# First slots of an attention and SwiGLU kernel: own buffers for weight chunks, and another placing of products

## The chip, the cores and the metric

The kernel runs on one core of a Trainium2 chip. The time is device microseconds of one execution, from its first to its last instruction. TensorE (PE) multiplies matrices, VectorE (DVE), ScalarE (ACT) and GpSimd (POOL) work elementwise, and SyncE (SP) issues most of the transfers. PEld is TensorE's loading of weights, which overlaps its matmuls.

## The reference

Two attention steps over 32 inducing points, then an RMS norm and a gated feed-forward network. Setup and reference, cut:

```python
B, N, m, C = (4, 12416, 32, 128)           # attention; d_ff = 1536, 49664 tokens in all
def mab(q, kv):
    s = scale * (q @ kv.transpose(0, 2, 1))
    s = s - s.max(-1, keepdims=True)
    a = np.exp(s)
    a /= a.sum(-1, keepdims=True) + 1e-09
    return a @ kv
h = mab(I, x)
y = mab(x, h)                              # reshaped to (49664, 128)
# ...
xn = y / np.sqrt(np.mean(y * y, axis=-1, keepdims=True) + 1e-06) * rms_g
g = xn @ w_gate
silu = g * (1.0 / (1.0 + np.exp(-g)))
return (silu * (xn @ w_val) @ w_out).astype(np.float32)
```

The three weight matrices arrive as 64-bit floats. The kernel turns them into 32-bit ones itself, in nine chunks of 128x512: (0,c) of the gate, (1,c) of the value, (2,c) of the output weights, c = 0, 1, 2.

## The kernel before

The second attention and the network are joined: the weights of the network's first layer are multiplied with h once per batch (the stacks sg and sv), so that a block of up to 512 tokens needs only its normalised attention weights a. A **unit** is such a block; a **slot** is one of its 12 groups of 128 hidden channels. There are 4 x 25 x 12 = 1200 slots. In a slot TensorE projects twice, ScalarE takes the silu, VectorE multiplies, and later TensorE adds the **product** with the output weights:

```python
def slot(j, products, steps, tanh):
    products(0)
    g = bank()
    nc.tensor.matmul(g[:, 0:T], sg[:, ts(j, P)], a[:, 0:T], start=True, stop=True)      # L681
    # ... silu on ScalarE: L689
    products(1)
    v = bank()
    nc.tensor.matmul(v[:, 0:T], sv[:, ts(j, P)], a[:, 0:T], start=True, stop=True)      # L692
    # ... VectorE multiplies silu with v: L698
    steps()
    if (b, u, j) in kinds:
        soon(1, lambda: three(j, t))
    else:
        plain.append(lambda: project(wo[:, j, :], t[:, 0:T]))
```

A **plain** product is one matmul of 32-bit floats (L617). A **three** splits both operands into parts and does three faster matmuls (L637, L639 and L617) after work on ScalarE, VectorE and GpSimd (L663 to L673). Two of the three add up in one PSUM bank, u3; when the last one of a unit is in, ScalarE copies it out (L642).

`steps()` does all other work of the kernel that has been given to this slot: rounding chunks, scores, exponentials, the sums of the next batch. In the first slots it is this:

```python
for k, one in ((1, (2, 1)), (5, (0, 2)), (8, (1, 2)), (11, (2, 2))):       # rounding of four chunks
    for j, name in ((0, "power"), (1, "power_number"), (1, "upper"), (2, "upper_number"), (2, "sign"), (3, "lower")):
        add(k + j, weight[one][name])
for k, *one in ((2, 0, 1), (4, 1, 1), (11, 0, 2), (13, 1, 2)):
    add(k, f["stack_of"], *one)        # L471: chunk times h, into a stack
    add(k, f["stack_low"], *one)
```

Rounding ends with `lower`: VectorE joins the parts (L281), GpSimd multiplies and writes the chunk (L283), and SP copies it to DRAM for later batches (L221). Where the chunk lies is chosen in `power`:

```python
if not c:
    t = silp.tile([P, 512], F32, name="silu") if i else halves.tile([P, 512], F32, name="lo")
    w0[i, c] = t[:]
else:
    if (0, 1) not in w0:
        w0["home"] = xnp.tile([P, 4, 512], F32, name="xn1")
    w0[i, c] = w0["home"][:, 2 * (c - 1) + i, :]
```

The places xn1 to xn4 hold rows of x before that. Later xn2, xn3 and xn4 hold the parts hi, lo and d of the threes.

Which products go into which slot, and which of them are threes, is planned ahead in `rehearse()`, which adds up fixed durations per engine (`run` puts work on an engine's clock) and only writes lists:

```python
def has(kind, by):
    return bool(queues[kind]) and queues[kind][0][0] <= by

def fill(to, until):
    while until > at["PE"] + 0.25:
        now = at["PE"] + 0.05
        kind = next((kind for kind in ("three", "plain") if has(kind, now)), None)
        if kind is None:
            break
        issue(kind, to)

# do(name), one step's cost
for e, us in zip(ENGINES, cost):
    if us:
        t = run(e, us, t, free[i]) if e == "PE" and i is not None else run(e, us, t)

# in a slot
least = 1 if near(b, k, 0, 4) or (b, u) == flat[-1] else RESERVE + 2 * near(b, k, -2, 0)     # RESERVE is 7
choose(second, min(2, max(0, split["all"] - least + 1)))
```

`choose` issues products while at least `least` are outstanding; `fill` issues more where TensorE would wait for a bank.

Of the kernel before, what the change touches and what calls it, by code (L numbers as in the profile page):

```python
# [23 lines left out]
def kernel(  # L24
# [189 lines left out]
    def rounding(i, c):  # L214


        st = {}

        def put():
            if i < 2:  # L220
                nc.sync.dma_start(out=w32[i][c][:], in_=st["dst"])  # L221
            if unread:
                fetch_raw(*unread.pop(0))

        def numbers(name, add, mul, engine):

            t, to = st[name], st[name] if name == "e" else st[name].bitcast(F32)
            if engine is nc.scalar and name == "e":
                nc.scalar.activation(to[:], t[:], AF.Relu, bias=bias, scale=mul)
            elif engine is nc.scalar:  # L230
                nc.scalar.activation(to[:], t[:], AF.Copy, bias=add, scale=mul)
            else:
                engine.tensor_scalar(out=to[:], in0=t[:], scalar1=mul, scalar2=add, op0=ALU.mult, op1=ALU.add)

        def power():
            if i < 2:
                if not c:
                    t = silp.tile([P, 512], F32, name="silu") if i else halves.tile([P, 512], F32, name="lo")
                    w0[i, c] = t[:]
                else:  # L240
                    if (0, 1) not in w0:
                        w0["home"] = xnp.tile([P, 4, 512], F32, name="xn1")
                    w0[i, c] = w0["home"][:, 2 * (c - 1) + i, :]
                dst = st["dst"] = w0[i, c]
            else:
                dst = st["dst"] = wo.rearrange("p j c -> p (j c)")[:, ts(c, 512)]
            if not wide:
                nc.sync.dma_start(out=dst if i < 2 else dst.rearrange("p (j c) -> p j c", c=C), in_=source(i, c))
                return
            words = raw[i, c].rearrange("p (f w) -> p f w", w=2)  # L250
            st["low"], st["high"] = words[:, :, 0], words[:, :, 1]
            e = st["e"] = work.tile([P, 512], I32, name="we", tag="work")
            nc.vector.tensor_scalar(out=e[:], in0=st["high"], scalar1=20, scalar2=0x7FF,
                                    op0=ALU.logical_shift_right, op1=ALU.bitwise_and)

        def power_number(engine=nc.scalar):
            if wide:
                e = st["e"]
                if engine is not nc.scalar:
                    nc.vector.tensor_scalar(out=e[:], in0=e[:], scalar1=896.0, scalar2=1151.0, op0=ALU.max, op1=ALU.min)  # L260
                numbers("e", -896.0 * (1 << 23), float(1 << 23), engine)

        def upper():
            if wide:
                f = st["f"] = outp.tile([P, 512], I32, name="o")
                nc.vector.tensor_scalar(out=f[:], in0=st["high"], scalar1=0xFFFFF, scalar2=None, op0=ALU.bitwise_and)

        def upper_number(engine=nc.scalar):
            if wide:
                numbers("f", 1.0, 2.0 ** -20, engine)  # L270

        def sign():
            if wide:
                e = st["e"]
                nc.vector.scalar_tensor_tensor(out=e[:], in0=st["high"], scalar=-(1 << 31), in1=e[:],
                                               op0=ALU.bitwise_and, op1=ALU.bitwise_or)

        def lower():
            if wide:
                e, f = st["e"], st["f"].bitcast(F32)  # L280
                nc.vector.scalar_tensor_tensor(out=f[:], in0=st["low"].bitcast(U32), scalar=2.0 ** -52, in1=f[:],  # L281
                                               op0=ALU.mult, op1=ALU.add)
                nc.gpsimd.tensor_tensor(out=st["dst"], in0=f[:], in1=e.bitcast(F32)[:], op=ALU.mult)  # L283
            put()

        return dict(locals())
# [516 lines left out]
    if B > 1:  # L803
        for _ in range(R):
# [7 lines left out]
            "power": (0, .45), "power_number": (0, 0, .63), "upper": (0, .6), "upper_number": (0, 0, .53), "sign": (0, .6),  # L812
            "lower": (0, .6, 0, 1.26), "stack_of": (.87, 0, .5), "stack_low": (0, .62), "split_wo": (0, 0, .7, 1.52)}
    BANKS = {"scores1", "sum_h", "max2", "max3", "fold_l", "turn_h", "square_h", "stack", "scores2", "square", "stack_of"}
    ENGINES = ("PE", "DVE", "ACT", "POOL")
    TAIL = {"PE": .17, "DVE": .09, "ACT": .11, "POOL": .04}
    MADE = {"sums": ((-.16,), (0, .6, .49), (0, 0, 0, 1.25)), "differences": ((-.16,), (0, 0, .53, 1.25), (0, 0, .52, 1.25))}
# [113 lines left out]
    def rehearse():  # L931

        at = dict.fromkeys(ENGINES, 0.0)
        free, open_banks = [0.0] * 5, {}
        taken = [0.0] * SILU
        queues, uses, later, left = {"plain": [], "three": []}, [0], [], {}
        split = {"out": 0, "u3": 0.0, "all": 0, "made": 0}

# [4 lines left out]
        def bank():  # L943
            return free.index(min(free))
# [2 lines left out]
            later.append([k, step])  # L947

        def has(kind, by):
            return bool(queues[kind]) and queues[kind][0][0] <= by  # L950

        def ready():
            return sum(one[0] <= at["PE"] for q in queues.values() for one in q)
# [1 line left out]
        def issue(kind, to):  # L955
            to.append(kind)
            t, unit, w = queues[kind].pop(0)[:3]
            split["all"] -= 1
            st = left[unit]
            if kind == "plain":  # L960
                end = run("PE", 0.858 * w, t)
            else:
                if st["three"] == 0:
                    run("PE", 0, split["u3"])
                end = run("PE", 0.697 * w, t)
                split["out"] -= 1
                split["made"] -= 1
                st["three"] += 1
                st["open"] -= 1
            st["left"] -= 1  # L970
            st["end"] = end
            if not st["left"] and st["all"]:
                close(unit, w)

        def close(unit, w):
            st = left[unit]
            if st["three"]:
                split["u3"] = run("ACT", 0.47 * w, st["end"])

            def finish():  # L980
                run("DVE", 0.6 * w, st["end"], split["u3"])
                soon(1, lambda: run("DVE", 0.63 * w))

            soon(1, finish)
# [19 lines left out]
                    break  # L1004
                issue(kind, to)

        def do(name):
            cost = COST.get(name, ())
            t = 0.0
            if name == "turn_z" or name == "stack_low":  # L1010
                i, t = open_banks[name].pop(0)
                free[i] = run("DVE", 0.61, t)
                if name == "turn_z":
                    run("DVE", 0.63)
                return
            i = bank() if name in BANKS else None
            for e, us in zip(ENGINES, cost):
                if us:
                    t = run(e, us, t, free[i]) if e == "PE" and i is not None else run(e, us, t)
            if name in ("square", "stack_of"):  # L1020
                open_banks.setdefault("turn_z" if name == "square" else "stack_low", []).append((i, t))
                free[i] = 1e9
            elif i is not None:
                free[i] = t
# [24 lines left out]
        def slot(b, k, u, j, tanh):  # L1049
            w = per2[units[u][0]] * m / 512.0  # L1050
            st = left.setdefault((b, u), dict(left=NJ, three=0, open=0, all=False, slots=0, end=0.0))
            kind = decide(b, k, u, j)
            first, second = picks[b, k] = [], []
            gi = bank()
            fill(first, free[gi])
            g = run("PE", 0.2325 * w, free[gi])
# [1 line left out]
            if tanh:  # L1058
                silu = run("DVE", 0.6 * w, silu)
            free[gi] = silu  # L1060
            least = 1 if near(b, k, 0, 4) or (b, u) == flat[-1] else RESERVE + 2 * near(b, k, -2, 0)
            choose(second, min(2, max(0, split["all"] - least + 1)))
            if kind != "sums":
                uses[0] += 1
# [12 lines left out]
            while any(not one[0] for one in later):  # L1077
                one = next(one for one in later if not one[0])
                later.remove(one)
                one[1]()  # L1080
            names = [step.__name__ for step, _ in given(b, k, u, j)]
            for name in names:
                if name in ("exp1_of", "exp2") and k in plans[b][1]:
                    run("ACT", 1.28)
                do(name)
            if near(b, k, 2, 3):
                run("ACT", 1.28)
            if kind:
# [23 lines left out]
            st["slots"] += 1  # L1112
            if st["slots"] == NJ:
                st["all"] = True
                if not st["left"]:
                    close((b, u), w)

# [7 lines left out]
    for b in range(B):  # L1125
# [3 lines left out]
        for k, (u, j) in slots(b):  # L1129

            def steps():

                for one in waiting:
                    one[0] -= 1
                while any(not one[0] for one in waiting):
                    one = next(one for one in waiting if not one[0])
                    waiting.remove(one)
                    one[1]()
                for step, args in given(b, k, u, j):
                    step(*args)  # L1140
                if j == (6 if (b, u) == (0, R - 1) else 2) and (b or u > 1) and (b, u) in after:
                    gather(*after[b, u])

            def products(some):
                for kind in picks[b, k][some]:
                    (plain if kind == "plain" else kara).pop(0)()

            if u not in unit:
# [36 lines left out]
```

## Time and profile before

| | |
|---|---|
| time, median of 3 runs | 1638.86 us (1637.6 to 1640.44) |
| span of the profiled execution | 1635.7 us |
| granted TensorE clock | 1.00 |
| first slot's first projection | 55.12 us after the start |
| scores in the steps of slot 18 | 84.67 us |

Busy columns of a window are time in which an engine had an instruction open; for TensorE the ends are modelled and overlap, so the spacing of starts tells its work better. A releaser in brackets is the instruction whose end came last before the waiting one began; it is inferred.

### The profile page before, as it was taken

Reading aid. Unit: us, or ns where it says so; the run is one execution under the profiler, and the core shown is the slowest. Engines: PE = TensorE matmul, PEld = TensorE weight load, DVE = VectorE, ACT = ScalarE, POOL = GpSimd, SP = SyncE. Lnnn points to the kernel's source line nnn. Section 1 sums busy time; section 2 is a strip of 40 time slices with the busy share of each in tenths; the row PEclk is TensorE's granted clock in tenths of the full one; section 3 lists DMA queues with packets and bytes.
Section 4 is the critical chain, followed back from the end, with each engine's and each line's share of the span. In section 5 each row is a group of like instructions: output and inputs, shape, how many; then the busy total and the mean of one; then the engine's idle time right before and its main releaser. Section 6 shows DMA issues by size and latency. Waiting matters only on the chain.

```text
span 1635.7 us, 25441 instructions
## 1 busy us (share of the span) xinstructions
PE 1608.4 (98%) x7086; PEld 1084.5 (66%) x7086; DVE 1444.4 (88%) x2506; ACT 1246.0 (76%) x2285; POOL 1217.5 (74%) x979
## 2 busy tenths in 40 slices
PE   8899999999999999999999999999999999999998
PEld 6546666766676666765667666676567776677776
DVE  4878988899899997889899998789989999999997
ACT  4567888767787778777778787777778788778786
POOL 1348895878588886688767897577858878878876
PEclk9999999999999999999999999999999999999999
DMA  6455534433454241624335324253221122112211
GB/s 260 90 72 81 90 62 85 102 90 63 65 88 69 40 88 26 135 58 103 63 67 84 57 39 87 49 131 77 51 38 29 29 40 38 34 35 38 39 36 27
DMA packets 389181, 112.52 MB, mean 69 GB/s; under 512 B 365072, under 2 KB 369712, under 8 KB 386480
## 3 DMA queue, kind: packets, MB, share of 16 engines
q1 hardware_dynamic: 388304, 110.82, 34.6%
q8 instruction: 56, 0.92, 0.2%
q14 instruction: 85, 0.70, 0.2%
q10 hardware_dynamic: 736, 0.08, 0.0%
HBM read 53.95 MB, written 27.00 MB: 49 GB/s over the span
## 4 chain that ended last, share of the span: by engine, by line
PE 85%; DVE 4%; issue 3%; ACT 2%; POOL 2%; DMA 1%; SPq 0%; DVEq 0%; ACTq 0%; POOLq 0%
PE acc L617 31%; PE gv L681 16%; PE gv L692 15%; PE u L637 9%; PE u L639 9%; PE gv L326 3%; PE gv L503 1%; DVE gv L698 1%; PE gv L382 1%; ACT silu L689 1%; DVE u L698 1%; POOL rs L520 1%; POOL xn L673 1%; DVE xn L664 1%; PE gv L457 0%
## 5 line engine op out<-in xcount | busy, mean ns | idle before, releaser
L673 POOL TENSOR_TENSOR xn<-xn,xn 128x512 fp32r<-128x512 f32 (+2 forms) x706 | 872.0, 1255 | 305.9 <-DVE xn L664 169.5
L689 ACT ACTIVATE silu<-gv 128x512 f32<-128x512 f32 (+2 forms) x1186 | 691.5, 586 | 271.9 <-PE gv L681 242.5
L692 PE MATMUL gv<-a,sv 128*128 128x512 f32 (+2 forms) x1188 | 634.9, 534 | 2.4 <-ACT silu L689 2.2
L681 PE MATMUL gv<-a,sg 128*128 128x512 f32 (+2 forms) x1188 | 489.6, 412 | 1.9 <-ACT silu L689 0.8
L617 PE MATMUL acc<-u,wo 128*128 128x512 f32 (+2 forms) x988 | 489.5, 580 | 0.0
L698 DVE TENSOR_TENSOR u<-silu,gv 128x512 f32<-128x512 f32 (+1 forms) x619 | 407.3, 664 | 53.9 <-PE gv L692 33.3
L698 DVE TENSOR_TENSOR gv<-silu,gv 128x512 f32<-128x512 f32 (+2 forms) x567 | 378.5, 669 | 77.0 <-PE gv L692 55.7
L664 DVE SCALAR_TENSOR_TENSOR xn<-xn,gv 128x512 fp32r<-128x512 f32 (+2 forms) x568 | 373.1, 657 | 9.0 <-ACT xn L663 6.2
L663 ACT ACTIVATE xn<-gv 128x512 fp32r<-128x512 f32 (+2 forms) x568 | 332.2, 585 | 41.3 <-DVE gv L698 31.2
L681 PEld LDWEIGHTS gv<-a,sg 128*128 128x128 f32 x1188 | 223.7, 188 | 187.2 <-ACT silu L689 40.4
L692 PEld LDWEIGHTS gv<-a,sv 128*128 128x128 f32 x1188 | 223.7, 188 | 142.6 <-issue 48.9
L617 PE MATMUL acc<-xn,more 128*128 128x512 f32 (+2 forms) x706 | 275.1, 390 | 6.1 <-POOL xn L673 2.9
L637 PE MATMUL u<-xn,xn 128*128 128x512 f32 (+2 forms) x706 | 272.9, 387 | 0.9 <-ACT o L642 0.7
L617 PEld LDWEIGHTS acc<-u,wo 128*128 128x128 f32 x988 | 184.6, 188 | 46.3 <-issue 9.4
L668 POOL TENSOR_TENSOR xn<-u,xn 128x512 fp32r<-128x512 f32 (+1 forms) x138 | 177.3, 1285 | 5.4 <-ACT xn L667 5.4
L639 PE MATMUL u<-xn,xn 128*128 128x512 f32 (+2 forms) x413 | 159.8, 387 | 0.1
L617 PEld LDWEIGHTS acc<-xn,more 128*128 128x128 f32 x706 | 132.5, 188 | 40.8 <-POOL xn L673 13.4
L637 PEld LDWEIGHTS u<-xn,xn 128*128 128x128 f32 x706 | 132.7, 188 | 31.2 <-issue 4.6
L639 PE MATMUL u<-xn,more 128*128 128x512 f32 (+2 forms) x293 | 113.3, 387 | 0.0
L667 ACT ACTIVATE xn<-u 128x512 fp32r<-128x512 f32 (+1 forms) x138 | 87.0, 630 | 30.0 <-DVE u L698 23.1
L520 POOL TENSOR_TENSOR rs<-ms,mhalf 128x16 f32<-128x16 f32 (+2 forms) x28 | 75.9, 2710 | 25.2 <-DVE ms L515 24.8
L639 PEld LDWEIGHTS u<-xn,xn 128*128 128x128 f32 x413 | 77.5, 188 | 17.5 <-POOL xn L668 0.5
(151 smaller groups left out, 1092.2 us busy)
## 6 DMA issues: line engine op xcount, KB each, us to landing
out_dram<-o SPq DMA_DIRECT2D x320, 64.0 KB, 2.0
xT<-in_x_dram SPq DMA_DIRECT2D x60, 256.0 KB, 5.1
xn<-in_x_dram SPq DMA_DIRECT2D x60, 256.0 KB, 4.9
a<-hi SPq DMA_DIRECT2D x156, 64.0 KB, 2.0
a<-lo SPq DMA_DIRECT2D x156, 64.0 KB, 2.0
xn<-in_x_dram SPq DMA_DIRECT2D x5, 1024.0 KB, 10.2
xn<-w SPq DMA_DIRECT2D x18, 256.0 KB, 3.5
out_dram<-o SPq DMA_DIRECT2D x64, 60.0 KB, 2.0
```

Source lines behind the costliest of these rows:

```text
L520: nc.gpsimd.tensor_tensor(out=rs, in0=st["ms"], in1=mhalf[rows, 0:n], op=ALU.pow)
L617: nc.tensor.matmul(acc[:, 0:T], lhsT, rhs, start=st["left"] == NJ, stop=st["left"] == 1)
L637: nc.tensor.matmul(ups[:, 0:T], weight_of(0, j), hi, start=st["k"] == nk, stop=False)
L639: nc.tensor.matmul(ups[:, 0:T], weight_of(1, j), lo, start=False, stop=not st["k"])
L663: nc.scalar.activation(hi, v, AF.Copy, scale=(1.0 - 2.0 ** -13) * 2.0 ** -12)
L664: nc.vector.scalar_tensor_tensor(out=lo, in0=hi.bitcast(F32), scalar=-4096.0, in1=v, op0=ALU.mult, op1=ALU.add)
L668: nc.gpsimd.tensor_tensor(out=lo, in0=v, in1=d.bitcast(F32), op=ALU.subtract)
L673: nc.gpsimd.tensor_tensor(out=d, in0=hi.bitcast(F32), in1=lo.bitcast(F32), op=ALU.subtract)
L681: nc.tensor.matmul(g[:, 0:T], sg[:, ts(j, P)], a[:, 0:T], start=True, stop=True)
L689: nc.scalar.activation(sl[:, 0:T], g[:, 0:T], AF.Silu)
L692: nc.tensor.matmul(v[:, 0:T], sv[:, ts(j, P)], a[:, 0:T], start=True, stop=True)
L698: nc.vector.tensor_tensor(out=t[:, 0:T], in0=sl[:, 0:T], in1=v[:, 0:T], op=ALU.mult)
```

## The change

It gives each of the four later gate and value chunks a buffer of its own. Before slot 16 of the first batch, products are issued from three outstanding on instead of seven. The plan now knows when a step's operand is made (`AFTER`, `done`), and in front of a step's matmul it places products until the operand is due; the kernel issues these right ahead of that step. The plan also takes ScalarE's copy of u3 where the last three of a unit is issued, and holds a unit's first three back until that copy is over. No instruction is added or taken out by the placing; only order and the choice between plain and three can change.

The diff, cut:

```diff
         def power():
             if i < 2:
-                if not c:
-                    t = silp.tile([P, 512], F32, name="silu") if i else halves.tile([P, 512], F32, name="lo")
-                    w0[i, c] = t[:]
-                else:
-                    if (0, 1) not in w0:
-                        w0["home"] = xnp.tile([P, 4, 512], F32, name="xn1")
-                    w0[i, c] = w0["home"][:, 2 * (c - 1) + i, :]
+                t = (xnp.tile([P, 512], F32, name=f"xn{2 * c - 1 + i}") if c else
+                     silp.tile([P, 512], F32, name="silu") if i else halves.tile([P, 512], F32, name="lo"))
+                w0[i, c] = t[:]
# ... (AFTER, done, rounded)
         def has(kind, by):
-            return bool(queues[kind]) and queues[kind][0][0] <= by
+            if not queues[kind]:
+                return False
+            t, unit = queues[kind][0][:2]
+            if kind == "three" and not left[unit]["three"]:
+                t = max(t, split["u3"])
+            return t <= by
# ... issue(): a three
-                if st["three"] == 0:
-                    run("PE", 0, split["u3"])
                 end = run("PE", 0.697 * w, t)
# ...
+                st["end"] = end
+                copy(st, w)
# ...
+        def copy(st, w):
+            if st["all"] and st["three"] and not st["open"] and "u3" not in st:
+                st["u3"] = split["u3"] = run("ACT", 0.47 * w, st["end"])
+
         def close(unit, w):
             st = left[unit]
-            if st["three"]:
-                split["u3"] = run("ACT", 0.47 * w, st["end"])
# ... do()
-            t = 0.0
+            t = done.get(args if name == "stack_of" else AFTER.get(name), 0.0)
             i = bank() if name in BANKS else None
             for e, us in zip(ENGINES, cost):
+                if us and e == "PE":
+                    t = max(t, free[i])
+                    fill(to, t)
                 if us:
-                    t = run(e, us, t, free[i]) if e == "PE" and i is not None else run(e, us, t)
+                    t = run(e, us, t)
+            done[rounded[step] if step in rounded else name] = t
# ... slot()
-            least = 1 if near(b, k, 0, 4) or (b, u) == flat[-1] else RESERVE + 2 * near(b, k, -2, 0)
+            least = (1 if near(b, k, 0, 4) or (b, u) == flat[-1] else 3 if not b and k < 2 * NJ - 8 else
+                     RESERVE + 2 * near(b, k, -2, 0))
# ... the kernel's own loop
-                for step, args in given(b, k, u, j):
+                for n, (step, args) in enumerate(given(b, k, u, j)):
+                    products(n + 2)
                     step(*args)
```

More of the change, by code (lines that the diff above doesn't have):

```diff
@@ L814 @@
     BANKS = {"scores1", "sum_h", "max2", "max3", "fold_l", "turn_h", "square_h", "stack", "scores2", "square", "stack_of"}
+    AFTER = {"max2": "max1", "max3": "max2", "fold_l": "exp1_of", "turn_h": "divide", "square_h": "turn_h", "square": "turn_a",
+             "sum_h": "turn_e", "scores1": "turn_x", "stack": "turn_h", "root": "scale", "apply": "root"}
     ENGINES = ("PE", "DVE", "ACT", "POOL")
@@ L934, in rehearse @@
         free, open_banks = [0.0] * 5, {}
-        taken = [0.0] * SILU
+        taken, done = [0.0] * SILU, {}
+        rounded = {weight[one]["lower"]: one for one in chunks}
         queues, uses, later, left = {"plain": [], "three": []}, [0], [], {}
@@ L973, in issue @@
                 close(unit, w)
+        def copy(st, w):
+            if st["all"] and st["three"] and not st["open"] and "u3" not in st:
+                st["u3"] = split["u3"] = run("ACT", 0.47 * w, st["end"])
         def close(unit, w):
             st = left[unit]
-            if st["three"]:
-                split["u3"] = run("ACT", 0.47 * w, st["end"])
             def finish():
-                run("DVE", 0.6 * w, st["end"], split["u3"])
+                run("DVE", 0.6 * w, st["end"], st.get("u3", 0.0))
                 soon(1, lambda: run("DVE", 0.63 * w))
@@ L1005, in fill, with do @@
                 issue(kind, to)
-        def do(name):
+        def do(step, args, to):
+            name = step.__name__
             cost = COST.get(name, ())
-            t = 0.0
             if name == "turn_z" or name == "stack_low":
@@ L1052, in slot @@
             kind = decide(b, k, u, j)
-            first, second = picks[b, k] = [], []
+            first, second = [], []
+            picks[b, k] = {0: first, 1: second}
             gi = bank()
@@ L1080, in slot @@
                 one[1]()
-            names = [step.__name__ for step, _ in given(b, k, u, j)]
-            for name in names:
-                if name in ("exp1_of", "exp2") and k in plans[b][1]:
+            for n, (step, args) in enumerate(given(b, k, u, j)):
+                if step.__name__ in ("exp1_of", "exp2") and k in plans[b][1]:
                     run("ACT", 1.28)
-                do(name)
+                do(step, args, picks[b, k].setdefault(n + 2, []))
             if near(b, k, 2, 3):
@@ L1114, in slot @@
                 st["all"] = True
+                copy(st, w)
                 if not st["left"]:
@@ L1138, in steps @@
                     one[1]()
-                for step, args in given(b, k, u, j):
+                for n, (step, args) in enumerate(given(b, k, u, j)):
+                    products(n + 2)
                     step(*args)
@@ L1144, in products @@
             def products(some):
-                for kind in picks[b, k][some]:
+                for kind in picks[b, k].get(some, ()):
                     (plain if kind == "plain" else kara).pop(0)()
```

## The prediction

> **What bounds the kernel now.** I read the page first, then TensorE's busy time by stage, then the waits of the stage with the largest gap, then the timelines of the engines around that gap. The page's first part names the bound, and group 5 gives the count of one kind of work that I need later:
>
> ```profile
> PE 1608.4 (98%) x7086; PEld 1084.5 (66%) x7086; DVE 1444.4 (88%) x2506; ACT 1246.0 (76%) x2285; POOL 1217.5 (74%) x979
> ...
> L637 PE MATMUL u<-xn,xn 128*128 128x512 f32 (+2 forms) x706 | 272.9, 387 | 0.9 <-ACT o L642 0.7
> ```
>
> TensorE leaves 27 us of 1635.7 idle. Nothing that only shifts work between VectorE, ScalarE and GpSimd can pay unless it fills some of these 27 us; otherwise the number of TensorE passes has to change. 706 of the 1200 products are done in three fast passes and the other 494 in one slow one. Busy time by stage (columns: window, its length, then busy us and instruction count of PE, PEld, DVE, ACT, POOL, clock, DMA share, GB/s):
>
> ```profile
> 67.00:69.00 2.00, 2.00 (x8) 1.03 (x6) 2.00 (x4) 1.29 (x3) 0.00 (x0) 1.00 1.16 135
> 69.00:71.00 2.00, 0.68 (x3) 0.19 (x1) 1.66 (x5) 1.31 (x3) 0.00 (x0) 1.00 1.13 179
> 71.00:73.00 2.00, 0.00 (x0) 0.00 (x0) 2.00 (x4) 0.90 (x2) 1.21 (x1) 1.00 0.00 1
> 200.00:1600.00 1400.00, 1391.43 (x5937) 943.45 (x5936) 1261.80 (x2172) 1095.78 (x2008) 1091.26 (x867) 1.00 0.33 63
> 1600.00:1636.00 36.00, 29.77 (x139) 23.17 (x137) 26.13 (x52) 20.87 (x47) 21.37 (x22) 0.98 0.18 29
> ```
>
> Over 1400 us the middle wastes 8.6 us; one hole at 69 to 73 us wastes almost half of that at a stroke; the tail wastes 6.2, and the change does not aim at it. The timelines of TensorE, VectorE, GpSimd and the DMA queue's issuer show what the hole is (start, duration, then idle before it and its releaser in brackets):
>
> ```profile
> 69.28 0.40 PE L692 MATMUL gv<-a,sv 128*128 128x512 f32 x1
> 73.39 1.13 PE L471 MATMUL gv<-xn,hg 128*128 128x512 f32 x2 [3.71 <-POOL xn L283]
> ...
> 68.63 0.69 DVE L281 SCALAR_TENSOR_TENSOR o<-sc,o 128x512 f32<-128x512 uint32 x1
> ...
> 71.79 1.55 POOL L283 TENSOR_TENSOR xn<-o,we 128x512 f32<-128x512 f32 x1 [6.66 <-DVE u L698]
> 75.53 1.29 POOL L283 TENSOR_TENSOR xn<-o,we 128x512 f32<-128x512 f32 x1 [2.19 <-DMA w<-xn]
> ...
> 66.86 1.83 SPq L221 DMA_DIRECT2D w<-xn  x1
> ```
>
> L471 multiplies weight chunk (0,2), and GpSimd wrote that chunk only from 71.79 on, though VectorE had its input at 68.63 + 0.69 = 69.32. The page names a VectorE product as releaser, but nothing in lower() reads that product. What fits is the copy of the previous chunk out of the same buffer: issued at 66.86 behind four x loads, and of the w copies the slowest took 4.7 us to land, 66.86 + 4.7 = 71.56. The next chunk, at 75.53, is put down to such a copy by name. So the hole is a buffer wait of 71.79 - 69.32 = 2.5 us, followed by 1.55 us of GpSimd work.
>
> [...] nothing ran in the 3.7 us, though VectorE had made nine of the products by 68.7 and only five were issued, so four stood ready. [...] Here the w copies landed in 2.0 (least) to 4.7 us (most). [...] L281 took 1.16 us at 72.73, while GpSimd worked, against 0.69 at 68.63; so rounding chunks earlier does not come quite free. [...] in the first slots VectorE is the bound (busy 2.00 of 2.00 in several windows), afterwards TensorE.
>
> **The ruler for TensorE.** The busy column counts modelled ends that overlap, so I count work by the spacing of starts. In the chain of waits:
>
> ```profile
> 74.75 0.86 PE acc L617 x2
> 75.61 0.23 PE gv L692
> 75.84 0.24 PE gv L681
> 76.08 0.86 PE acc L617 x2
> ```
>
> A projection is 0.233 us, a slow product 0.86, a chunk product (L471 x2) 0.86. By the same spacing a fast product is three passes, 0.70. From the first slot (55.12) to the scores of slot 18 (84.67) are 29.55 us. In them the timeline has 38 projections (8.84), 4 chunk products (3.44) and 12 slow products (10.3): 22.6 us of work, 7.0 idle. By part: 55.12 to 69.51 (the end of the last projection) 14.4 us with 24 projections, 2 chunk and 5 slow products = 11.6 of work, idle 2.8; the hole 3.9; 73.39 to 84.67 idle 0.3.
>
> **The change part by part.**
> 1. *Own buffers.* Chunks (0,1), (1,1), (0,2), (1,2) go to xn1 to xn4 instead of four quarters of xn1. The x rows that lay there were read for the last time at 38 us, so no new wait at this end. At the other end xn2 to xn4 become hi, lo and d of the fast products; the first of these is written after slot 26, past 100 us, when the copies at 73 to 77 us have landed. The wait of 2.5 us goes: GpSimd at 69.4, the chunk ready near 70.9 instead of 73.35. The 2.2 us wait at 75.53 goes too. No instruction is added.
> 2. *Products ahead of late operands.* In front of a step's matmul the schedule now puts ready products until the operand is due. In the rest of the hole (69.51 to 70.9, 1.4 us) one or two products fit: 0.86 or 1.7 us. The order alone changes, the count does not. In the middle I find little for this part: the waits of TensorE itself between 200 and 1600 us, 7.5 us in all, are at L617, L692, L681 and L637, none at scores, squares or sums. I allow 0.3 us.
> 3. *Three outstanding, not seven, before slot 16.* Up to four slow products are done earlier, 4 x 0.86 = 3.4 us, into time that is idle. It adds no gain to the idle time itself; it is what can fill it. It also has a price: after slot 16 seven are wanted again, so four slots run without a product, at 0.47 + half a score step (0.5) = 1.0 us of TensorE against 0.6 + 0.6 = 1.2 of VectorE. That may cost 4 x 0.2 = 0.8; fills take some of it, I choose 0.4.
> 4. *The plan's copy of u3, its tests of readiness and operand times.* These move ScalarE's L642 nowhere; they only alter which kind of product is chosen in which slot. One product changed from slow to fast is 0.86 - 0.70 = 0.16 us of TensorE. I cannot derive the direction; ten either way are 1.6 us. This is my widest term.
>
> Is VectorE in the way? From its first product at 56.28 it has to finish slot 15: 16 products x 0.6 = 9.6, four and a half chunks of rounding, about 9.9, four stack halves x 0.7 = 2.8: 22.3 us, so not before 78.6. In the run before, this product started at 82.12. TensorE by then has 32 projections (7.4), 4 chunk products (3.4) and 13 slow products (11.2) = 22.0, 55.12 + 22.0 = 77.2. VectorE therefore holds TensorE up by some 1.5 us in any case.
>
> **The sum.** Idle before 7.0. After: 2.8 becomes about 2.0, since the first product exists only from 57.0 on; the hole 3.9 becomes 0.3; the last part 0.3 becomes 0.5 as VectorE comes close. 7.0 - 2.8 = 4.2, less 0.4 for the refill, plus 0.3 in the middle: 4.1 us. 1638.9 - 4.1 = **1634.8**, rounded to the ratio 0.9975.
>
> **Rivals.**
> *A: the hole only moves.* With the buffer wait gone, VectorE's queue of rounding, stack halves and products is the bound up to slot 15, and the gain is what VectorE gives, not TensorE. For it: VectorE at 2.00 of 2.00 around the hole. Against it: in the hole VectorE worked on and was then short of work after 75 us, with gaps of 0.64 us per slot. It would leave 1.5 to 2.5 us: 1636.5 to 1637.4.
> *B: the new plan shifts the kinds.* Operand times for root and apply make GpSimd look later in the plan, so fewer products are given to it; 15 fewer fast products cost 2.4 us and leave 1637. Or TensorE looks less held up, with the reverse: 1632. For it: every later slot is planned anew. Against it: the loads, limits and reserve that decide are unchanged.
> *C: the seam comes first.* The chain runs from 113.5 to 133 us through GpSimd's root (2.9 us) and DMA to the next operand, and TensorE waits 0.4 there. If that chain does not start 4 us earlier along with the slots, the gain is lost there. Against it: it hangs on slots too. Then 1638 to 1639.
>
> **Range and chances.** A pulls up by 2, B goes 2 to 3 either way, C up by 4 with little weight; the three runs before spread over 2.8 us. So 1630.5 to 1638.5. Two per cent are 33 us, more than all of TensorE's idle time: faster 0.01, same 0.98, slower 0.01.
>
> **What would show it.** L283 for the third chunk right after its L281; the wait at L471 gone or under 1 us; slow products ahead of that L471; 84.67 reached 4 us earlier; L637 still near 706. Wrong: the wait at L471 still over 2 us (the copy was not the cause), L637 under 690 or over 720, or gaps in the middle over 11 us.

## The result, and the profile after

| | before | after |
|---|---|---|
| time, median | 1638.86 us | 1623.18 us (1623.0 to 1623.49, 5 runs) |
| ratio, 95% interval | | 0.9904 (0.989 to 0.9919) |
| span of the profiled execution | 1635.7 us | 1621.7 us |
| products done as threes | 706 of 1200 | 705 of 1200 |

The change took off 15.7 us, not 4.1. The number of threes is the same but for one, so TensorE has the same work. The first part of the page, and then TensorE's busy time in the stretches that were shown of before:

```profile
PE 1604.3 (99%) x7085; PEld 1085.6 (67%) x7085; DVE 1444.6 (89%) x2504; ACT 1238.3 (76%) x2285; POOL 1217.7 (75%) x979
...
L633 PE MATMUL u<-xn,xn 128*128 128x512 f32 (+2 forms) x705 | 272.4, 386 | 0.0
```

```profile
67.00:69.00 2.00, 2.00 (x8) 1.14 (x7) 1.78 (x3) 1.68 (x4) 0.00 (x0) 1.00 0.98 129
69.00:71.00 2.00, 2.00 (x9) 1.14 (x7) 2.00 (x5) 0.93 (x2) 1.16 (x1) 1.00 1.09 201
71.00:73.00 2.00, 2.00 (x7) 1.04 (x6) 2.00 (x4) 1.78 (x4) 0.18 (x1) 1.00 0.46 173
200.00:1600.00 1400.00, 1395.71 (x5967) 950.82 (x5966) 1270.19 (x2182) 1096.25 (x2022) 1100.85 (x875) 1.00 0.32 62
1600.00:1622.00 22.00, 15.80 (x79) 11.93 (x77) 12.28 (x28) 8.94 (x24) 8.68 (x11) 1.00 0.19 29
```

The hole at 69 to 73 us is gone, the tail still wastes 6.2 us, and the middle wastes 4.3 us by this column where it wasted 8.6. The timelines of VectorE, GpSimd and TensorE at the place of the hole (all line numbers of the changed kernel are 4 lower there):

```profile
69.02 0.68 DVE L277 SCALAR_TENSOR_TENSOR o<-sc,o 128x512 f32<-128x512 uint32 x1
...
69.84 1.34 POOL L279 TENSOR_TENSOR xn<-o,we 128x512 f32<-128x512 f32 x1 [4.31 <-DVE o L277]
74.08 1.34 POOL L279 TENSOR_TENSOR xn<-o,we 128x512 f32<-128x512 f32 x1 [2.89 <-PE gv L688]
...
70.93 0.80 PE L688 MATMUL gv<-a,sv 128*128 128x512 f32 x1
71.56 1.02 PE L467 MATMUL gv<-xn,hg 128*128 128x512 f32 x2
...
75.47 1.12 PE L467 MATMUL gv<-xn,hg 128*128 128x512 f32 x2 [0.23 <-POOL xn L279]
```

GpSimd writes chunk (0,2) 0.14 us after VectorE's end of it (69.02 + 0.68 = 69.70), and TensorE goes from a projection into the chunk product without a wait.

Where the rest came from is best seen slot by slot. All 1200 starts of the gate projection are in both traces; "gained" is how much earlier this start is than in the run before, each counted from the start of its own span:

| at slot | 0 | 12 | 24 | 42 | 60 | 300 | 600 | 900 | 1199 |
|---|---|---|---|---|---|---|---|---|---|
| gained, us | -0.4 | 1.9 | 4.7 | 4.7 | 7.2 | 8.3 | 10.0 | 11.5 | 14.0 |

Counted from the first slot, 5.0 us come by slot 24, where all of the predicted gain but 0.3 us was to come, another 2.5 by slot 60, and then about 1.1 to 2.5 us in each batch of 300 slots. The remaining 15.7 - 14.0 = 1.7 us are not in these two profiles.

### The profile page after: what moved, and what is told of

It is laid out like the page before. It is cut to its first block, busy times and chain, and to the rows that moved or that the text cites. A ratio compares the mean times of both kernels' runs of the same rounds, so it can differ in the third digit from the quotient of the medians.

```text
span 1621.7 us, 25435 instructions
## 1 busy us (share of the span) xinstructions
PE 1604.3 (99%) x7085; PEld 1085.6 (67%) x7085; DVE 1444.6 (89%) x2504; ACT 1238.3 (76%) x2285; POOL 1217.7 (75%) x979
## 4 chain that ended last, share of the span: by engine, by line
PE 94%; DVE 1%; ACT 1%; issue 1%; POOL 0%; DVEq 0%; ACTq 0%
PE acc L613 35%; PE gv L677 18%; PE gv L688 16%; PE u L635 10%; PE u L633 10%; PE gv L322 3%; PE gv L499 1%; PE gv L378 1%; DVE gv L694 1%; ACT silu L685 1%; PE gv L453 0%; DVE xn L660 0%; PE gv L467 0%; DVE o L621 0%; POOL xn L279 0%
## 5 line engine op out<-in xcount | busy, mean ns | idle before, releaser
L669 POOL TENSOR_TENSOR xn<-xn,xn 128x512 fp32r<-128x512 f32 (+2 forms) x705 | 870.9, 1255 | 268.6 <-DVE xn L660 156.8
L613 PE MATMUL acc<-u,wo 128*128 128x512 f32 (+1 forms) x990 | 490.8, 581 | 0.0
L694 DVE TENSOR_TENSOR u<-silu,gv 128x512 f32<-128x512 f32 (+2 forms) x621 | 407.7, 663 | 51.7 <-PE gv L688 32.3
L613 PE MATMUL acc<-xn,more 128*128 128x512 f32 (+2 forms) x705 | 273.6, 388 | 3.0 <-DVE o L621 2.6
L613 PEld LDWEIGHTS acc<-u,wo 128*128 128x128 f32 x990 | 184.9, 188 | 46.7 <-issue 9.1
L664 POOL TENSOR_TENSOR xn<-u,xn 128x512 fp32r<-128x512 f32 (+2 forms) x139 | 178.6, 1285 | 41.6 <-ACT xn L663 41.6
L613 PEld LDWEIGHTS acc<-xn,more 128*128 128x128 f32 x705 | 132.4, 188 | 33.5 <-POOL xn L669 5.7
L663 ACT ACTIVATE xn<-u 128x512 fp32r<-128x512 f32 (+2 forms) x139 | 87.4, 629 | 36.6 <-DVE u L694 32.4
```

What stands on the lines that cost most here:

```text
L613: nc.tensor.matmul(acc[:, 0:T], lhsT, rhs, start=st["left"] == NJ, stop=st["left"] == 1)
L663: nc.scalar.activation(d, v, AF.Copy, scale=1.0 - 2.0 ** -13)
L664: nc.gpsimd.tensor_tensor(out=lo, in0=v, in1=d.bitcast(F32), op=ALU.subtract)
L669: nc.gpsimd.tensor_tensor(out=d, in0=hi.bitcast(F32), in1=lo.bitcast(F32), op=ALU.subtract)
L694: nc.vector.tensor_tensor(out=t[:, 0:T], in0=sl[:, 0:T], in1=v[:, 0:T], op=ALU.mult)
```

## The experiments

Times are medians, with the ratio to the kernel before as measured beside them. "Gained" is as in the table above. The start of the first slot itself differs by up to 1.2 us between the profiles (54.29 to 55.51 us), whatever was edited; so where two versions are close, "gained from the first slot" leaves this difference out.

**One part alone on the kernel before.** First the own buffers:

```diff
-                    w0[i, c] = w0["home"][:, 2 * (c - 1) + i, :]
+                t = (xnp.tile([P, 512], F32, name=f"xn{2 * c - 1 + i}") if c else ...)
```

> The kernel before with nothing but the four own buffers; the plan and the order of every instruction stay. Theory (the copy of chunk (1,1) held the shared buffer): GpSimd writes chunk (0,2) within 0.5 us of VectorE's end of it, the wait before the chunk product shrinks from 3.9 to about 1.4 us, time about 2.5 us under before (1636). Rival (GpSimd waited for something else): the wait stays at 3.9 us and the time at 1638.9.

Measured 1635.83 us, ratio 0.9983 (0.9976 to 0.9989): 2.9 us. GpSimd's timeline around the hole:

```profile
69.66 1.33 POOL L279 TENSOR_TENSOR xn<-o,we 128x512 f32<-128x512 f32 x1 [4.32 <-PE gv L677]
```

It ran 2.1 us earlier than in the run before and the spacing of starts ahead of the chunk product exceeded its usual value by 1.33 us instead of 3.89, as expected of a buffer held by the copy. But by slot 18 only 1.6 us of the gain were left: TensorE next had to wait about 0.6 us for the following chunk, which GpSimd began at 73.88, directly after VectorE's end of it at 73.06 + 0.68 = 73.74. The buffer is the cause of 2.5 us of the hole's length, and VectorE's pace limits what its removal alone brings.

With three outstanding products as well:

```diff
+            least = (1 if near(b, k, 0, 4) or (b, u) == flat[-1] else 3 if not b and k < 2 * NJ - 8 else ...)
```

> The kernel before with own buffers and three outstanding products before slot 16; no other change to the plan. Theory (the first slots are worth 4.7 of the 14 us by these two and the placing ahead of chunk products): slot 24 begins 3.5 to 4.5 us earlier than before, nothing more is gained after it, time about 1635. Rival (an earlier start also removes the later waits, because the whole pipeline of operands moves): slot 60 and later keep on gaining, time under 1630.

Measured 1632.09 us, ratio 0.9961 (0.9947 to 0.9974): 6.6 us, more than the 4 or so expected. Gained 5.3 us at slot 24 and 5.5 at the end: a start that is earlier removes nothing later. From the first slot to slot 24 it is 5.0 us, as in the changed kernel. So these two edits, without any placing inside steps, do all of the change's work in the first slots. Why the median fell by 1.1 to 1.4 us more than the profile is told below, with the clock.

The third part, the plan's account of u3:

```diff
+        def copy(st, w):
+            if st["all"] and st["three"] and not st["open"] and "u3" not in st:
+                st["u3"] = split["u3"] = run("ACT", 0.47 * w, st["end"])
```

> The kernel before with only the plan's new account of the copy of u3 (copy at the last three, first three of a unit held back until the copy is over). Theory R (the gain after slot 24 comes from GpSimd's operand times for root and apply): within 1.5 us of before, 1637.5 to 1640, and TensorE's waits for a three's last operand at the third slot of every eighth unit stay at 0.3 to 0.5 us. Rival U (the u3 account makes the gain): 6 to 9 us under before, 1630 to 1633, and these waits vanish.

Measured 1635.56 us, ratio 0.9979 (0.9972 to 0.9986): 3.1 us, between the two theories. Gained nothing before slot 54, 2.9 us at the end. TensorE's waits for a three's last operand stayed. The number of threes is 705.

The fourth, the operand times of root and apply:

```diff
+    AFTER = {"root": "scale", "apply": "root"}
...
+            t = done.get(AFTER.get(name), 0.0)
```

> The kernel before with one addition to the plan: root may not begin before scale is done, apply not before root. Theory R: the waits for a three's last operand at the third slot after a seam (0.3 to 1.1 us, about ten of them) vanish, the plan gives GpSimd less there, time 3 to 7 us under before, 1632 to 1636. Rival U: order nearly that of before, time 1637.5 to 1640.

Measured 1634.17 us, ratio 0.9975 (0.9966 to 0.9984): 4.5 us. Here the waits for the last operand did vanish at slots 42, 170, 470 and 770, and the longer ones of the last batch (0.34 to 0.47 us); those of 0.28 us stayed. This version also makes 709 threes instead of 706, which by 0.16 us each is about 0.5 of the 4.5 us. Both theories held for a part; neither is the whole.

The fifth, products in front of late operands, with shared buffer, seven outstanding and the old accounts:

```diff
+                if us and e == "PE":
+                    t = max(t, free[i])
+                    fill(to, t)
```

> The kernel before with nothing but products placed ahead of late operands (all operand times in the plan except root's and apply's); shared buffer, seven outstanding, old u3 account. The order differs from before in the first slots alone. Theory F (the idle time of the first slots can be filled by either means, placing or a smaller reserve): the hole is filled with three or four products, 3 to 5 us under before, 1634 to 1636, nothing gained after slot 24. Rival (the placing needs the own buffers, since the shared one delays the chunk whatever TensorE does meanwhile): under 2 us, 1637 to 1639.

Measured 1634.22 us, ratio 0.9971 (0.996 to 0.9983): 4.5 us, as theory F has it. Gained 3.0 us at slot 24 and 3.0 at the end. TensorE's timeline shows three plain products in the hole and what is left of it:

```profile
69.22 0.39 PE L692 MATMUL gv<-a,sv 128*128 128x512 f32 x1
69.45 2.74 PE L617 MATMUL acc<-u,wo 128*128 128x512 f32 x6
73.33 1.13 PE L471 MATMUL gv<-xn,hg 128*128 128x512 f32 x2 [1.15 <-POOL xn L283]
```

**One part taken out of the changed kernel.** Without the placing:

```diff
-                    fill(to, t)
```

> The changed kernel without the products in front of late operands; it is in effect the kernel before with own buffers, three outstanding, the u3 account and the operand times. The parts that were tried alone took off 6.6, 3.1 and 4.5 us. Theory S (these three add up, the placing within steps gives about nothing): 1624 to 1625.5, slot 24 as early as in the changed kernel. Rival P (the placing is what fills the first slots, as the change's name says): slot 24 comes 1.4 us or more later, 1626 or more.

Measured 1623.63 us, ratio 0.9909 (0.9895 to 0.9922). From the first slot to slot 24 it gained 5.0 us, as the changed kernel did. Theory S holds: once the other parts are in, the placing is worth nothing in the first slots. Over the whole kernel it is worth little: 0.45 us between medians that were not measured side by side, 0.8 us between the two profiles from the first slot on (14.3 against 13.5), all of it after slot 60.

```diff
-            least = (... else 3 if not b and k < 2 * NJ - 8 else RESERVE + 2 * near(b, k, -2, 0))
+            least = 1 if near(b, k, 0, 4) or (b, u) == flat[-1] else RESERVE + 2 * near(b, k, -2, 0)
```

> The changed kernel with seven outstanding products in the first slots as before; own buffers and placing stay. Theory S (own buffers alone gave 2.9 us, with three outstanding 6.6): 3 to 4 us over the changed kernel, 1626 to 1627, slot 24 later by as much. Rival P (placing within steps fills the hole whatever the reserve): under 1 us, 1623 to 1624.

Measured 1624.1 us, ratio 0.9911 (0.9897 to 0.9925): my expectation of 1626 to 1627 missed. From the first slot to slot 24 it gained 4.4 us, 0.7 less than the changed kernel. TensorE's timeline shows why it is not more:

```profile
69.67 0.39 PE L688 MATMUL gv<-a,sv 128*128 128x512 f32 x1
69.90 2.74 PE L613 MATMUL acc<-u,wo 128*128 128x512 f32 x6
72.47 1.02 PE L467 MATMUL gv<-xn,hg 128*128 128x512 f32 x2
```

With seven held back, three products were there to be placed ahead of the chunk product. Smaller reserve and placing are two ways to fill the same idle time, and either is nearly enough.

```diff
-                t = (xnp.tile([P, 512], F32, name=f"xn{2 * c - 1 + i}") if c else ...)
+                    w0[i, c] = w0["home"][:, 2 * (c - 1) + i, :]
```

> The changed kernel with the four chunks back in one buffer; the order of all instructions stays. Theory: the copy holds chunk (0,2) back by about 2.5 us again; three outstanding leaves few products to fill with and the order is fixed for the earlier chunk, so slot 24 comes 1.5 to 3 us later, 1625 to 1626. Rival (TensorE has enough to do in any case): under 0.7 us over the changed kernel.

Measured 1626.09 us, ratio 0.9922 (0.9909 to 0.9936). With the shared buffer back, the wait is back, smaller because nine products had been issued before it:

```profile
72.58 1.13 PE L471 MATMUL gv<-xn,hg 128*128 128x512 f32 x2 [1.42 <-POOL xn L283]
```

From the first slot to slot 24 this profile gained 3.9 us, 1.1 less than the changed kernel and not the 1.5 to 3 that I expected. Its five times part by the mean granted clock: 1624.62 us at 1.000, but 1626.74 and 1627.26 at 0.998. At 1.000 it is 1.4 us over the changed kernel, about half of the 2.9 us by which its median is over; the rest came with the clock, which the experiment with the hole takes up.

Next the two accounts of the plan:

```diff
-        def copy(st, w): ...
+            if st["three"]:
+                split["u3"] = run("ACT", 0.47 * w, st["end"])       # in close(), as before
```

> The changed kernel with the plan's old account of the copy of u3. Theory S: 2.5 to 4 us over the changed kernel, 1626 to 1627, all of it after slot 60, with the short waits of a value projection for a bank (0.28 to 0.67 us, near slots 139, 195, 439, 495) back. Rival (the root times alone already remove them): within 1 us of 1623.

Measured 1627.48 us, ratio 0.9931 (0.9919 to 0.9943): 4.3 us over the changed kernel, a little more than expected. Up to slot 60 it gained as much as the changed kernel (7.6 us from the first slot), and 4.8 us less by slot 1199, though it makes 709 threes. TensorE's waits from slot 42 to the tail have these lines for a value projection and for a three's first matmul (columns: who waited for whom, us in total, times, longest); in the changed kernel, shown further down, the first is 0.6 us and the second does not appear:

```profile
PE gv L688 <- ACT silu L685: 1.8, 6, 0.5
PE u L633 <- ACT o L638: 0.7, 2, 0.3
```

```diff
-             "sum_h": "turn_e", "scores1": "turn_x", "stack": "turn_h", "root": "scale", "apply": "root"}
+             "sum_h": "turn_e", "scores1": "turn_x", "stack": "turn_h"}
```

> The changed kernel without the two entries that make root wait for scale and apply for root; all other operand times stay. Theory S: 3 to 5 us over the changed kernel, 1626 to 1628, the waits for a three's last operand at slots 42 (1.1 us), 170, 470, 770 and in the last batch (0.3 to 0.5 us each) back. Rival (other operand times or the placing do it): these waits stay away and the time stays at 1623 to 1624.5.

Measured 1628.5 us, ratio 0.9939 (0.9925 to 0.9953). This is 5.3 us over the changed kernel. The waits for a three's last operand (L613 for L669) came back; the same stretch without root's times, and then in the changed kernel:

```profile
PE acc L613 <- DVE o L621: 2.7, 3, 0.9
PE acc L613 <- POOL xn L669: 2.6, 7, 0.9
PE gv L688 <- ACT silu L685: 0.6, 3, 0.2
```

```profile
PE acc L613 <- DVE o L621: 2.6, 3, 0.9
PE gv L688 <- ACT silu L685: 0.6, 3, 0.2
PE gv L677 <- DVE xn L660: 0.3, 2, 0.2
```

**Which half of the u3 account.**

```diff
+                st["end"] = end
+                copy(st, w)               # copy booked at the last three; a unit's first three is still a stall
```

> The kernel before with half of the plan's u3 account: the copy is booked at the last three of a unit; a unit's first three is still booked as a stall and not held back. (The other half alone leaves the order on TensorE row for row as before.) Theory: all of the 3.1 us of the full account comes from booking the copy where the kernel issues it, 1635 to 1636.5. Rival (both halves are needed): 1638 to 1639.

Measured 1636.58 us, ratio 0.9989 (0.9982 to 0.9995), against 0.9979 (0.9972 to 0.9986) for the whole account. The time lies just outside what was expected and the intervals overlap, so the times do not settle it. On the kernel before, the profiles leave about 0.9 us to the other half: the whole account gained 3.0 us from the first slot to the end, this half 0.4, and 1.65 of its loss is a half clock behind the hole (next experiment), which makes 2.1. In the changed kernel it is settled: built with only this half, it has on every engine the same instructions in the same order, so there the other half does nothing.

**Does the hole cost more than its own length?**

```diff
             ps = st["stack", i, c] = bank()
+            if (i, c) == (0, 2):
+                for _ in range(12):
+                    nc.tensor.matmul(ps[:, 0:P], ident[:], ident[:], start=True, stop=True)
```

> The kernel before with 12 small matmuls of the identity put ahead of chunk (0,2)'s product, into the bank that this product overwrites: about 2.9 us of work for TensorE inside the hole of 3.9 us, which moves no other instruction. Theory (the hole also costs TensorE's clock: in two of the profiles with the hole the granted clock is 0.50 for some 4 us after it, in others it is not): the clock stays at 1.00 after the hole, and the median falls by 0.7 to 1.5 us to 1637.2 to 1638 with a narrower spread of runs. Rival (the drop of the clock has nothing to do with idle time, or costs nothing in the median): 1638.2 to 1639.5, spread as before.

Measured 1637.09 us (1636.46 to 1637.86, 13 runs) beside 1638.49 us (1637.05 to 1640.47, 17 runs) for the kernel before; ratio 0.9992 (0.9984 to 1.0). Work without any use in the hole (2.94 us on TensorE from 69.49 us on, by the timeline) makes the kernel 1.4 us shorter and its spread 1.4 us instead of 3.4, with an interval that just touches 1. The times of the kernel before part by the clock. Of the 17 executions of the kernel before, the 4 with a mean granted clock of 1.000 took 1637.05 to 1637.52 us, the 9 with 0.999 took 1638.11 to 1638.84, and the 4 with 0.998 or 0.997 took 1638.96 to 1640.47. With the hole filled, 10 of 13 have 1.000 and none is under 0.999. The profile shows where the clock falls. Windows of the run with root's times alone, which has the hole too (clock is the third number from the end):

```profile
69.00:73.50 4.50, 0.88 (x3) 0.20 (x2) 4.16 (x8) 2.21 (x4) 1.32 (x1) 0.82 0.61 97
73.50:76.00 2.50, 2.41 (x4) 1.28 (x5) 0.93 (x2) 0.29 (x1) 0.29 (x2) 0.50 0.28 105
76.00:78.00 2.00, 2.00 (x4) 0.90 (x3) 0.69 (x1) 1.40 (x3) 1.02 (x1) 0.50 0.06 23
78.00:82.00 4.00, 4.00 (x12) 2.30 (x11) 2.95 (x5) 2.31 (x4) 0.00 (x0) 0.91 0.14 54
```

and the same stretches of the profiled run of before:

```profile
69.00:73.50 4.50, 0.79 (x4) 0.30 (x2) 4.16 (x8) 2.21 (x4) 1.55 (x1) 1.00 0.50 80
73.50:76.00 2.50, 2.50 (x8) 1.41 (x9) 1.47 (x4) 1.44 (x3) 0.47 (x1) 1.00 0.28 105
76.00:78.00 2.00, 2.00 (x7) 0.94 (x6) 1.83 (x4) 1.37 (x3) 0.83 (x1) 1.00 0.15 59
```

After the hole TensorE ran at half clock in the one and not in the other: the windows count 4 and 4 matmuls in the 4.5 us against 8 and 7. Counted from the first slot, slot 24 was 2.5 us later for it. The profiled run of before is the lowest of its times (1637.6 us), and its clock did not fall; so the medians hold some of this loss and the profile none. That accounts for the direction of the missing 1.7 us, and about 1.4 us of its size. It also is why own buffers, three outstanding or the placing alone took 1.0 to 1.5 us more off the median than off the profile: they shorten or fill the hole, and none of their executions has a mean clock under 0.999.

**One step further.**

```diff
-            if not st["left"]:
+            if not st["left"] and u == NU - 2:
+                finish()
+            elif not st["left"]:
                 soon(1, finish)
```

> The changed kernel with one line more: the last but one unit of a batch has its result added up in the slot of its last product and not one slot later. In the changed kernel TensorE still waits 1.05 us three times (slots 305, 605, 905) for VectorE to empty an accumulation bank (L621). Theory: these three waits shrink to under 0.3 us each, 2 to 2.5 us under the changed kernel, 1621. Rival (VectorE then waits for TensorE and the loss moves to the value products): within 0.5 us of 1623.2.

Measured 1622.18 us (1621.82 to 1622.27), ratio 0.9897 (0.9884 to 0.9911): 1.0 us under the changed kernel, which was not measured beside it. The profiles do not credit this to the edit. In this one the first slot itself starts 1.0 us earlier (54.52 against 55.48), where the edit changes nothing; from there to slot 1199 the two differ by 0.4 us. The three waits of 1.05 us are gone, but the start spacing shows 0.5 us ahead of a gate projection instead (slots 306, 606, 906) and 0.27 ahead of a value projection (310, 610, 910). So the loss mostly moved, as the rival has it, and a gain from this line is not shown.

## Why the prediction was wrong

**Right: the cause of the hole and the ruler.** The copy of the previous chunk held the buffer; own buffers alone brought GpSimd forward by 2.1 us. The predicted gain of 4.2 us up to slot 18 was nearly what came: the scores of slot 18 start 80.83 - 55.48 = 25.35 us after the first projection, 4.1 us less than the 84.60 - 55.12 = 29.48 that the same view has before, with 13 plain products in that stretch instead of 12, so 5.0 us with the extra product. VectorE's bound held as well: slot 15's product started at 79.36, and the bound was 78.6. (Before, it started at 80.79; the 82.12 that the prediction gives is slot 16's.) What closed the gap was not what part 2 said: not the placing, but the reserve of three. I had written that the reserve "adds no gain to the idle time itself"; it fills it as well as the placing does.

**Wrong: the middle.** The step that failed is in parts 2 and 4: "In the middle I find little", with 0.3 us allowed, and the new accounts of the plan as a matter of 0.16 us per changed product. The middle gave 14.0 - 4.7 = 9.3 us with the same number of threes. Two errors lie behind it.

The first is the size of what could be won. I took the waits of TensorE (7.5 us from 200 to 1600 us) and 1400 minus its busy time (8.6 us) for a ceiling, although I had written that modelled ends cover idle time. An excess of 1.13 us in the start spacing at slot 42 is listed as 0.85 us idle, and one of 0.28 us at slot 953 not at all. Measured by start spacing, as the excess over the usual spacing of an instruction behind the same two before it (usual is the lower fifth over these runs; excesses over 0.05 us, slots 24 to 1189):

| us lost just ahead of | before | after | root times alone | u3 account alone | after, no root times | after, old u3 |
|---|---|---|---|---|---|---|
| a three's last matmul | 9.1 | 4.2 | 4.9 | 8.8 | 8.7 | 4.9 |
| a value projection | 8.9 | 5.3 | 7.2 | 7.3 | 7.3 | 7.0 |
| a three's first matmul | 3.5 | 2.2 | 4.2 | 2.2 | 1.9 | 4.0 |
| all places | 64.4 | 55.0 | 59.4 | 60.5 | 60.2 | 60.1 |

64.4 - 55.0 = 9.4 us is the whole gain of the middle. The levels hang on which neighbours count as the same; the differences between columns hardly do. Some 31 us of every column lie between the equal matmuls of one step (sums, scores) and are the same in every version, so they may be that work's own spacing. With each such row of equal matmuls taken as one piece, the last row is about 32 us before and 22 after. The chances and the rivals should have been drawn over such a first column.

The second error is the kind of effect. I looked for a change in how many products are threes (rival B) and found no direction. What changed in the whole change is where they are (706 and 705); root's times alone gave 3 more of them, not fewer as rival B argued. GpSimd's timeline in the run before shows it at slots 38 to 45:

```profile
118.87 2.90 POOL L520 TENSOR_TENSOR rs<-ms,mhalf 128x16 f32<-128x16 f32 x1 [2.56 <-DVE ms L515]
121.85 1.05 POOL L524 TENSOR_TENSOR sc<-sc,rs 128x512 f32<-128x512 f32 x1
122.86 1.29 POOL L668 TENSOR_TENSOR xn<-u,xn 128x512 fp32r<-128x512 f32 x1
124.23 1.28 POOL L673 TENSOR_TENSOR xn<-xn,xn 128x512 fp32r<-128x512 f32 x1
125.45 1.29 POOL L668 TENSOR_TENSOR xn<-u,xn 128x512 fp32r<-128x512 f32 x1
126.83 1.29 POOL L673 TENSOR_TENSOR xn<-xn,xn 128x512 fp32r<-128x512 f32 x1
...
125.56 0.50 PE L617 MATMUL acc<-xn,more 128*128 128x512 f32 x1 [0.85 <-POOL xn L673]
...
133.04 0.47 PE L681 MATMUL gv<-a,sg 128*128 128x512 f32 x1 [0.38 <-DMA a<-lo]
```

GpSimd sat idle for 2.56 us ahead of root (L520), because scale on VectorE was late. The old plan booked root at once, thought GpSimd free too early by about those 2.56 us, and gave it two threes right behind. Their last operand (L673) came late, TensorE waited, and the seam's lo (L537) came only at 128.07, so the next unit's operand was late too. With root's times in the plan (the changed kernel):

```profile
117.18 1.05 POOL L520 TENSOR_TENSOR sc<-sc,rs 128x512 f32<-128x512 f32 x1
118.19 1.28 POOL L664 TENSOR_TENSOR xn<-u,xn 128x512 fp32r<-128x512 f32 x1
119.55 1.28 POOL L669 TENSOR_TENSOR xn<-xn,xn 128x512 fp32r<-128x512 f32 x1
120.79 1.28 POOL L533 TENSOR_TENSOR lo<-aT,hi 128x512 fp32r<-128x512 f32 x1
```

one three fewer stands there, lo follows 3.6 us after apply instead of 6.2 (120.79 - 117.18, 128.07 - 121.85), and both waits of TensorE are gone. That is rival C's chain, with the opposite sign: the seam was not in the way of the gain, it gave part of it. The same repeats at later seams, 0.3 to 0.5 us each (slots 170, 470, 770 and in the last batch).

The u3 account works on other places: with it a three's first matmul loses 1.3 to 1.8 us less and a value projection 1.6 to 1.7 less, in both comparisons of the table. In the changed kernel, what has to be right is the booking of the copy at the last three, where the kernel issues it. By which of the plan's decisions that removes the waits for a bank was not traced and stays open.

**The sum as measured.** Own buffers and three outstanding 6.6 us (5.2 in the profile, the rest loss of clock behind the hole), u3 account 3.1, root's times 4.5: 14.2 of 15.7. Taken out of the changed kernel, the last two cost 4.3 and 5.3, so they help each other by about 1 us. The placing adds 0.45 us by the medians and 0.8 by the profiles, none of it in the first slots.

## What to carry to other kernels

Where a kernel places its work by a plan of its own, an error in the plan's clocks can cost as much as a wait in the kernel (here 4.5 and 3.1 us beside a hole of 3.9): compare the plan's start of an operation with the trace's, above all where an engine is shown idle ahead of it, as GpSimd ahead of root. Measure what is to be won on TensorE by the spacing of starts, not by busy time or listed waits. And before crediting a mechanism, ask whether another part of the same change fills the same gap; here either of two nearly did.

## What the runs showed of the hardware

An idle gap of 3.7 us on TensorE cost more than itself in some executions. In the run with root's times alone the clock column of the windows shown with that experiment amounts to 6.8 us at 0.50: (1 - 0.82) x 4.50 x 2 = 1.6, then 2.5 and 2.0, then (1 - 0.91) x 4.00 x 2 = 0.7, so from about 71.9 us on. The product of chunk (0,2) took 2.08 us there by the timeline, against 1.13 in the run before. The run with half of the u3 account has 3.4 us by the same sum (1.25, 2.0 and 0.16), from about 74.75 us on:

```profile
69.00:73.50 4.50, 0.78 (x4) 0.34 (x3) 4.16 (x8) 2.21 (x4) 1.66 (x1) 1.00 0.46 80
73.50:76.00 2.50, 2.50 (x6) 1.04 (x6) 1.36 (x3) 1.50 (x3) 0.52 (x1) 0.75 0.28 105
76.00:78.00 2.00, 2.00 (x6) 1.28 (x4) 1.03 (x2) 0.97 (x3) 0.75 (x1) 0.50 0.19 75
78.00:82.00 4.00, 4.00 (x12) 2.08 (x12) 2.94 (x5) 2.13 (x4) 0.00 (x0) 0.98 0.08 28
```

The profiles of before and of the u3 account alone, which have the same hole, show 1.00 in all of these stretches. By slot 24 these two drops had cost 2.5 and 1.65 us.

The two falls do not stand at the same place in the hole. In the one TensorE was idle from 69.88 us to the fall at about 71.9 and then on to 73.59, when the chunk product began (73.59 - 3.71 = 69.88); in the other it was busy again in all of the stretch from 73.50 on, some 1.2 us before the fall. What decides whether and when the clock falls is not shown.

With the hole filled by the small matmuls, with own buffers alone, with the shared buffer put back and in the changed kernel, the clock is 1.00 in every window from 55 to 82 us. Other executions of the version with the shared buffer, where 1.42 us of the hole are left, have a mean clock of 0.998; where it fell in them is not on a trace.
